# Work of the second batch ordered behind the first batch's last fold in an attention, DFT and feed-forward kernel

## The chip, the cores and the metric

The kernel runs as one program on one core of one Trainium2 chip. The metric is the device time of one execution in microseconds (us); lower is better. The core has a matrix engine (TensorE, PE in the views), a vector engine (VectorE, DVE), a scalar engine (ScalarE, ACT), a general engine (GpSimd, POOL) and an engine that here only issues transfers (SyncE, SP). Each engine carries out its own instructions in order, and engines wait for one another at semaphores.

## The reference

What is computed, for 8 batches, 12 heads, 448 tokens and 64 values per head (768 values per token):

```
q_n, k_n = rmsnorm(q, g_q), rmsnorm(k, g_k)
scores = (q_n @ k_n^T) / sqrt(64);  attn = softmax(scores);  x = attn @ v    # 12 heads side by side: 448 x 768
mixed = real(fft(fft(x, axis=tokens), axis=values))
u = x + mixed;  un = (u - mean(u)) / sqrt(var(u) + 1e-6)
out = u + relu(un @ w_ch1) @ w_ch2                                           # 768 -> 3072 -> 768
```

The two weight matrices reach the kernel as 64-bit floats and are turned into 32-bit pieces on the chip.

## The kernel before, in words

Heads are worked on two at a time: six pairs per batch. For a batch, `aux(b)` does everything ahead of the feed-forward product, as a Python generator that yields after each small step:

- `transpose_pair(b, p)` loads a pair (tile `raw`), scales it by its norm in `norm_pair` (sums of squares `ss`, a power, and two multiplies into `qkn`) and turns it by matrix transposes (`qk` in PSUM) into the tiles `QT` and `KD`. In names of tiles the pair and the part follow: `qk_1_0` is part 0 of pair 1.
- Scores `S_p_c_h`, their row extremes `mn` on DVE, exponentials `P` on ACT with row sums `sums`, transposes `pt` and `rem`, the copies `T`, the product `av` with the values, and the division (`rs`, `rt`), which ends in the transposed result `xT`.
- `fold(b, p, ...)` takes the sums and differences of pairs `p` and `p + 3` that the three-point stage of the Fourier transform needs: `eo`, `sd`, `eo` again, and, for the last fold of batch 0, six operations (two halves e = 0, 1, three each) that update the three tiles `eo_0`, `eo_1` and `tot`.
- `spectral(b, ...)`: four products `y_r_s` of 6 matmuls each from `eo_0`, `eo_1`, `tot` and a constant table; each is split into a rounded part by ACT and a rest by DVE (`Y`); then products `ab`, their sums and differences `smdf`, the residual sum `u` with statistics `st`, and the normed, transposed input `un` of the feed-forward product. `y_0_*` needs only half e = 0 for the first three of its 6 matmuls and half e = 1 for the other three; so do `y_1_*`.

`ffn(b)` then multiplies: 24 blocks `h` of 18 matmuls (L1039), each ending in `hs`, and after every four of them six blocks `o` of 12 matmuls (L1060), added into `acc`. In the first pass the weights are converted as they come in: a transfer `dbl`, two ACT operations, three DVE operations (L785, L789, L793, tile `mag`, or `mage` in the start-up), an addition on POOL (L797), a rounding copy on ACT (L802) and a DVE subtraction (L803, tiles `w`, `w2e`).

The order of work is set in three layers. While batch 0 is prepared no feed-forward work exists yet; the last lines of `spectral_block` walk through `aux(0)` and, once its list `mixing` is filled, take one step of `second = aux(1)` behind each step of it, at most `AHEAD = 14`. Afterwards `merge` mixes the rest of `aux(1)` into the first feed-forward pass in proportion to declared costs (`RATIO_FIRST`), and so on for each later batch. Last, a scheduler of the compiler, which simulates a timeline, takes this program and decides the final order on each engine and which PSUM bank a tile gets (tiles are not tied to fixed buffers here). An order can be forced on it by `order(...)`, which adds a dependency without a semaphore between two instructions of one engine. All V, A and G operations go through the recorder at L115, so they all have that line in the profile; operations of the weight conversion on DVE do not.

Of the kernel before, what the change touches and what calls it, by code (L numbers as in the profile page):

```python
# [16 lines left out]
ALU = mybir.AluOpType  # L17
# [7 lines left out]
NPAIR = H // 2  # L25
# [22 lines left out]
HALF_SCORES = range(NPAIR + 1)  # L48
PACE = 3
LAG = 3  # L50
LAST_JOINT = 2

MIN_HIGH = float(np.uint32(0x38000000).view(np.float32))
# [38 lines left out]
def spectral_block(ctx, tc, q, k, v, g_q, g_k, w1, w2, d1, d2, out, nb=B):  # L92
# [8 lines left out]
    )  # L101

    given = {}

    class Recorded:

# [4 lines left out]
        def __getattr__(self, name):  # L111
            emit = getattr(self.engine, name)

            def call(*args, **kwargs):
                ins = emit(*args, **kwargs)  # L115
                given.setdefault(ins.ins.engine, []).append(ins)
                return ins

            return call

    V, A, G = Recorded(nc.vector), Recorded(nc.scalar), Recorded(nc.gpsimd)
# [45 lines left out]
        V.tensor_tensor(out=o, in0=a, in1=b_, op=ALU.subtract)  # L167

    def add(o, a, b_):
        V.tensor_tensor(out=o, in0=a, in1=b_, op=ALU.add)  # L170

    def rows_of(n):

# [84 lines left out]
    def norm_pair(b, p):  # L258
        raw, vt = loaded.pop((b, p))
        qk = sb.tile([C, 2, NC, 2, D], F32, tag="qk", name=f"qkn{b}_{p}", bufs=1)  # L260
        sq = qk.rearrange("t i c h d -> t (i c h) d")
        flat = raw.rearrange("t i h c d -> t (i h c) d")
        nth = b * NPAIR + p
        if b < EARLY:
            A.activation(sq, flat, AF.Square)
        else:
            G.tensor_tensor(out=sq, in0=flat, in1=flat, op=ALU.mult)
        ss = sb.tile([C, 16], F32, tag="ss", name=f"ss{b}_{p}")
        V.tensor_reduce(ss, sq, axis=AX.X, op=ALU.add)
        V.tensor_scalar(  # L270
            out=ss, in0=ss, scalar1=1.0 / D, scalar2=EPS, op0=ALU.mult, op1=ALU.add
        )
        G.tensor_tensor(out=ss, in0=ss, in1=nhalf[:C], op=ALU.pow)
        for i in range(2):
            V.tensor_tensor(
                out=qk[:, i].rearrange("t c h d -> t h c d"),
                in0=raw[:, i],
                in1=ss[:, 8 * i : 8 * i + 8]
                .rearrange("t (h c) -> t h c", h=2)[:, :, :, None]
                .broadcast_to([C, 2, NC, D]),  # L280
                op=ALU.mult,
            )
        if plain(b, p):
            return qk, vt
        vhl = sb.tile([128, 4, 4, D], F32R, tag="vhl", name=f"vhl{b}_{p}", bufs=1)
        A.copy(vhl[:, :, ::3], vt)
        V.tensor_tensor(
            out=vhl[:, :, 1:3], in0=vt, in1=vhl[:, :, ::3], op=ALU.subtract
        )
        return qk, vhl  # L290
# [16 lines left out]
    def transpose_pair(b, p):  # L307

        if b >= nb or (b, p) in ready:
            return  # L310
        load_pair(b, p)
        qk, vhl = norm_pair(b, p)
        load_pair(*next_pair(b, p))
        yield 0

        if plain_s(b, p):
            T = []
            for i, tag in enumerate(("QT", "KD")):
                pt = bank(QK_BANKS[b > 0][i], f"qk{b}_{p}_{i}")
                for c in range(NC):  # L320
                    nc.tensor.transpose(
                        pt[:, c * C : (c + 1) * C],
                        qk[:, i, c].rearrange("t h d -> t (h d)"),
                        ident[:C, :C],
                    )
                t = sb.tile([128, S], F32, tag=tag, name=f"{tag}{b}_{p}")
                if i == 0:
                    A.copy(t, pt[:, :S])
                else:
                    A.activation(t, pt[:, :S], AF.Copy, scale=gneg)  # L330
                T.append(t)
                yield 420
            ready[b, p] = T[0], T[1], vhl
            return

        QT = sb.tile([128, 900], F32R, tag="QT", name=f"QT{b}_{p}")[:, : 2 * S].rearrange(
            "r (h t) -> r h t", h=2
        )
        KD = sb.tile([128, 900], F32R, tag="KD", name=f"KD{b}_{p}")[:, : 2 * S].rearrange(
            "r (h t) -> r h t", h=2  # L340
        )
        for i in range(2):
            pt = bank(QK_BANKS[b > 0][i], f"qk{b}_{p}_{i}")
            for c in range(NC):
                nc.tensor.transpose(  # L345
                    pt[:, c * C : (c + 1) * C], qk[:, i, c].rearrange("t h d -> t (h d)"),
                    ident[:C, :C],
                )
            src = pt[:, :S]
            if half_s(b, p):  # L350
                if i == 0:
                    A.copy(QT[:, 0], src)
                    sub(QT[:, 1], src, QT[:, 0])
                else:
                    A.activation(KD[:, 0], src, AF.Copy, scale=gneg)
                    V.scalar_tensor_tensor(
                        out=KD[:, 1], in0=src, scalar=gneg, in1=KD[:, 0],
                        op0=ALU.mult, op1=ALU.subtract,
                    )
            elif i == 0:  # L360
                A.copy(QT[lo, 0], src[lo])
                A.copy(QT[hi, 1], src[hi])
                sub(QT[hi, 0], src[lo], QT[lo, 0])
                sub(QT[lo, 1], src[hi], QT[hi, 1])
            else:
                for h, sl in enumerate((lo, hi)):
                    A.activation(KD[sl, h], src[sl], AF.Copy, scale=gneg[sl])
                    V.scalar_tensor_tensor(
                        out=KL[sl, h], in0=src[sl], scalar=gneg[sl], in1=KD[sl, h],
                        op0=ALU.mult, op1=ALU.subtract,  # L370
                    )
                A.copy(KD[hi, 0], KD[lo, 0].bitcast(F32))
                A.copy(KD[lo, 1], KD[hi, 1].bitcast(F32))
            yield 420

        ready[b, p] = QT, KD, vhl
# [156 lines left out]

    xTs = {}
    mixing = []

    def attention(b, EO):

# [28 lines left out]
        for n, x in enumerate(values):  # L567
            yield x
            if b == 1 and n == 4:
                fold(b, 1, xTs[b], EO)  # L570
                yield 2000
        fold(b, 2, xTs[b], EO)
        yield 3000 if b == 1 else 0


# [4 lines left out]
    def fold(b, p, xT, EO):  # L580
# [18 lines left out]
        if b == 0 and p == 2:  # L599
            for e in range(2):  # L600
# [5 lines left out]
                    out=a_, in0=two, scalar=-0.5, in1=a_, op0=ALU.mult, op1=ALU.add  # L606
                )
                sub(b_, b_, two)
                add(c_, c_, two)
            return  # L610
        twice = eo.rearrange("r i (e t) -> r (i e) t", e=2)
        add(twice[:, :, :N1], once[:, :, :N1], once[:, :, NT - 1 : N1 - 2 : -1])
        sub(twice[:, :, N1:], once[:, :, :N2], once[:, :, NT - 1 : N1 - 1 : -1])
# [142 lines left out]
    def aux(b):  # L756

        EO, uns[b] = [], {}
        yield from attention(b, EO)
        yield from spectral(b, xTs[b], EO, uns[b])  # L760
# [352 lines left out]
    load_pair(0, 0)  # L1113
    warm()
    second = aux(1)
    ahead = iter(range(AHEAD if nb > 1 else 0))
    for n, _ in enumerate(aux(0)):
        if n == DFT_STEP:
            load_dft()
        if mixing:  # L1120
            for _ in range(1):
                if next(ahead, None) is not None:
                    next(second)
        if n:
            convert_some(CONVERT_EARLY)
    starting[0] = False
# [32 lines left out]
```

## Time and profile before

| what | value |
|---|---|
| time, median of 3 runs | 2143.0 us (2142.21 to 2144.28) |
| the profiled execution: time, span of its trace | 2144.78 us, 2143.0 us |
| mean granted TensorE clock (share of full) | 0.984 |
| PE busy | 2074.9 us, 97% of the span |
| DVE busy | 1548.4 us, 72% |
| ACT busy | 1023.3 us, 48% |
| POOL busy | 342.1 us, 16% |

The span is what the trace of one execution covers; what lies around it, 1.78 us here, belongs to the time too. The busy shares are means over the whole span: in the slices of the page PE is at 7 or 8 tenths in the first four fortieths (about 214 us) and at 9 or more nearly everywhere behind them.

### The profile page before, as it was taken

Reading aid. Unit: us, or ns where it says so; the run is one execution under the profiler, and the core shown is the slowest. Engines: PE = TensorE matmul, PEld = TensorE weight load, DVE = VectorE, ACT = ScalarE, POOL = GpSimd, SP = SyncE. Lnnn points to the kernel's source line nnn. Section 1 sums busy time; section 2 is a strip of 40 time slices with the busy share of each in tenths; the row PEclk is TensorE's granted clock in tenths of the full one; section 3 lists DMA queues with packets and bytes.
Section 4 is the critical chain, followed back from the end, with each engine's and each line's share of the span. In section 5 each row is a group of like instructions: output and inputs, shape, how many; then the busy total and the mean of one; then the engine's idle time right before and its main releaser. Section 6 shows DMA issues by size and latency. Waiting matters only on the chain.

```text
span 2143.0 us, 31181 instructions
## 1 busy us (share of the span) xinstructions
PE 2074.9 (97%) x11256; PEld 1846.7 (86%) x11256; DVE 1548.4 (72%) x2948; ACT 1023.3 (48%) x2182; POOL 342.1 (16%) x182
## 2 busy tenths in 40 slices
PE   7877999999999999999999999999999999999998
PEld 4546888889999999999999999999999989999998
DVE  6788888977885878757886778858787578764122
ACT  6857876446542555335542455425553455422100
POOL 3324433311110101001110111101010011000000
PEclk9987999999999999999999999999999999999999
DMA  6538876776566855658555765667556674458874
GB/s 185 184 97 297 275 263 220 269 237 189 174 180 189 235 165 174 187 183 231 156 175 176 240 181 169 179 194 229 166 177 189 190 206 138 152 174 253 233 251 150
DMA packets 283550, 423.86 MB, mean 198 GB/s; under 512 B 181075, under 2 KB 200516, under 8 KB 283396
## 3 DMA queue, kind: packets, MB, share of 16 engines
q1 hardware_dynamic: 278962, 419.75, 63.8%
q10 hardware_dynamic: 4434, 2.11, 0.4%
q8 instruction: 90, 1.47, 0.3%
q14 instruction: 64, 0.52, 0.1%
HBM read 362.01 MB, written 65.31 MB: 199 GB/s over the span
## 4 chain that ended last, share of the span: by engine, by line
PE 81%; DVE 6%; DMA 5%; ACT 3%; issue 2%; POOL 1%; SPq 1%; DVEq 0%; POOLq 0%; ACTq 0%
PE h L1039 29%; PE o L1060 29%; PE S L409 5%; PE av L521 4%; PE pt L509 4%; DMA dbl<-w 2%; PE y L646 2%; PE qk L345 1%; DMA w<-w 1%; PE av L483 1%; DMA ur<-u_dram 1%; ACT P L115 1%; PE oT L996 1%; PE x L677 1%; PE un L908 1%
## 5 line engine op out<-in xcount | busy, mean ns | idle before, releaser
L1039 PE MATMUL h<-unT,w 128*128 128x448 f32 x3456 | 792.0, 372 | 3.4 <-DVE unT L115 1.4
L1060 PE MATMUL o<-hs,w 128*128 128x448 f32 x3456 | 786.4, 371 | 3.1 <-DVE acc L115 1.5
L1039 PEld LDWEIGHTS h<-unT,w 128*128 128x128 f32 x3456 | 638.9, 189 | 57.8 <-DVE unT L115 1.7
L1060 PEld LDWEIGHTS o<-hs,w 128*128 128x128 f32 x3456 | 635.9, 188 | 58.6 <-issue 3.4
L115 ACT ACTIVATE P<-S,mn 112x448 f32<-112x448 f32 x384 | 244.1, 638 | 232.6 <-DVE mn L115 226.7
L115 DVE TENSOR_REDUCE mn<-S 112x1 f32<-112x448 f32 x384 | 232.8, 616 | 47.9 <-PE S L409 38.3
L115 ACT ACTIVATE hs<-h 128x448 fp32r<-128x448 f32 x192 | 104.2, 543 | 299.0 <-PE h L1039 298.2
L115 DVE TENSOR_TENSOR acc<-o,acc 128x448 f32<-128x448 f32 (+1 forms) x240 | 146.9, 614 | 126.6 <-PE o L1060 125.0
L115 DVE SCALAR_TENSOR_TENSOR hs<-h,hs 128x448 fp32r<-128x448 f32 x192 | 119.0, 620 | 139.7 <-ACT hs L115 138.6
L115 POOL TENSOR_TENSOR qkn<-raw 112x1024 f32<-112x1024 f32 x36 | 68.6, 1904 | 679.3 <-PE qk L345 606.1
L115 POOL TENSOR_TENSOR ss<-ss,nhalf 112x16 f32<-112x16 f32 x48 | 142.6, 2972 | 190.2 <-DVE ss L115 167.2
L115 ACT CAST T<-pt 128x448 fp32r<-128x448 f32 x216 | 113.2, 532 | 107.3 <-PE pt L509 105.0
L521 PE MATMUL av<-T,vhl 128*128 128x448 f32 x432 | 151.0, 382 | 0.0
L115 DVE TENSOR_TENSOR T<-pt,T 128x448 fp32r<-128x448 f32 x216 | 131.4, 616 | 25.8 <-ACT T L115 24.7
L115 DVE TENSOR_SCALAR P<-P,sm 112x448 f32<-112x448 f32 x288 | 126.6, 479 | 3.8
L409 PE MATMUL S<-KD,QT 128*112 128x448 f32 x328 | 126.5, 386 | 0.6 <-ACT P L115 0.5
L509 PE MATMUL pt<-ident,P 112*128 112x112 f32 x864 | 124.8, 259 | 0.0
L409 PE MATMUL S<-rounded,QT 128*112 128x448 f32 x328 | 119.9, 366 | 0.0
L509 PEld LDWEIGHTS pt<-ident,P 112*128 112x128 f32 x864 | 103.5, 140 | 16.3 <-DVE R L115 0.3
L115 POOL TENSOR_TENSOR rstd<-st,nhalf 112x1 f32<-112x1 f32 (+2 forms) x32 | 20.2, 632 | 507.7 <-DVE st L115 507.7
L797 POOL TENSOR_TENSOR mag<-mag,dbl 128x768 uint32<-128x768 uint32 (+1 forms) x33 | 75.9, 2301 | 140.6 <-DVE mag L793 93.5
L521 PEld LDWEIGHTS av<-T,vhl 128*128 128x128 f32 x432 | 80.9, 188 | 8.3
(120 smaller groups left out, 2501.4 us busy)
## 6 DMA issues: line engine op xcount, KB each, us to landing
w<-w SPq DMA_DIRECT2D x192, 768.0 KB, 4.9
w<-w SPq DMA_DIRECT2D x288, 512.0 KB, 4.4
dbl<-w SPq DMA_DIRECT2D x20, 768.0 KB, 4.7
dbl<-w SPq DMA_DIRECT2D x13, 1024.0 KB
raw<-q SPq DMA_DIRECT2D x96, 112.0 KB, 3.8
raw<-k SPq DMA_DIRECT2D x96, 112.0 KB, 4.6
values<-v SPq DMA_DIRECT2D x96, 96.0 KB, 4.2
u_dram<-u SPq DMA_DIRECT2D x24, 336.0 KB, 3.8
```

What stands on the lines that cost most here:

```text
L115: ins = emit(*args, **kwargs)
L345: nc.tensor.transpose(pt[:, c * C : (c + 1) * C], qk[:, i, c].rearrange("t h d -> t (h d)"), ident[:C, :C],)
L409: ins = nc.tensor.matmul(s_, QT[:, h, cs], K[:, h], start=step == 0, stop=step == 1)
L483: nc.tensor.matmul(av[:, :S], vhl[:, 3 * h + j].rearrange("s h d -> s (h d)"), T, start=h + j == 0, stop=False,)
L509: nc.tensor.transpose(pt[:, c * C : (c + 1) * C], Pc[c][:, 512 * h + j * 128 : 512 * h + (j + 1) * 128], ident[:C, :C],)
L521: nc.tensor.matmul(av[:, :S], lv, T[:, i], start=(j == 0 and i == 0), stop=False)
L646: nc.tensor.matmul(o, src[:, par, t0 : t0 + n], D1[:, ri, par, cols], start=i != 1, stop=i != 0,)
L677: nc.tensor.transpose(xp[:n, i * 128 : (i + 1) * 128], src[:, 3 * half + i], ident)
L797: behind(nc.gpsimd.tensor_tensor(out=bits, in0=bits, in1=low, op=ALU.add))
L908: nc.tensor.transpose(pt[:, OFFS[i] : OFFS[i] + LENS[i]], uns[i][:, p * 128 : (p + 1) * 128], ident[: LENS[i], : LENS[i]],)
L1039: pace(nc.tensor.matmul(o, w[:, a, c], unT[c][:, z], start=n == 0, stop=n == 17))
L1060: pace(nc.tensor.matmul(o, w[:, a, f], hs[4 * g + f][:, z], start=n == 0, stop=n == 11))
```

## The change

Four things are edited.

- A dictionary `fences` holds, per engine, an instruction behind which every recorded instruction of that engine is ordered while it is set. Since `fold` now returns its last addition, which is on DVE, only DVE instructions are held.
- The loop over `aux(0)` counts the steps of `second` that it has taken. Up to `BEFORE_FOLD = 7` are taken ahead of batch 0's last fold, and the others behind it, under the fence.
- `norm_pair` becomes a generator; for the pair number `SPLIT_NORM = 7` (batch 1, pair 1, its second) it yields between the power and the two multiplies into `qkn`, so that these fall into a step of their own.
- The four tiles for converted values (slot "M") of the title are the same number in both kernels.

```diff
+SPLIT_NORM = NPAIR + 1
+BEFORE_FOLD = 7
...
             def call(*args, **kwargs):
                 ins = emit(*args, **kwargs)
+                if ins.ins.engine in fences:
+                    order(
+                        ins, fences[ins.ins.engine],
+                        mybir.DependencyClass.NoSync, mybir.DependencyReason.DATA,
+                    )
...
         G.tensor_tensor(out=ss, in0=ss, in1=nhalf[:C], op=ALU.pow)
+        if nth == SPLIT_NORM:
+            yield 0
...
-        qk, vhl = norm_pair(b, p)
+        qk, vhl = yield from norm_pair(b, p)
...
-        fold(b, 2, xTs[b], EO)
+        last = fold(b, 2, xTs[b], EO)
+        if b == 0:
+            folded.append(last)
...
+    stepped = [0]
     ahead = iter(range(AHEAD if nb > 1 else 0))
...
         if mixing:
-            for _ in range(1):
+            if folded:
+                fences[folded[0].ins.engine] = folded[0]
+            if folded or stepped[0] < BEFORE_FOLD:
                 if next(ahead, None) is not None:
+                    stepped[0] += 1
                     next(second)
+            fences.clear()
```

What the scheduler makes of it: the order of the two kernels is the same up to about the end of batch 0's attention and again from the first feed-forward pass's last `o` blocks to the end. It differs between. Three places follow. In names the prefixes are those explained above; the numbers at the end of a name only keep tiles apart.

**DVE at the fold.** First the kernel before, from the extremes of `S_0_2_0` (batch 1, pair 0) to the start of the fold's six last operations.

```order
L115 TENSOR_REDUCE mn_0_2_1310<-S_0_2_0_1311 112x1
L789 TENSOR_SCALAR mage_1270<-mage_1270 128x768
L115 TENSOR_TENSOR qkn_1_1290<-raw_1_1091,ss_1_1292 112x2x4x64 x2
L115 TENSOR_TENSOR xT_281<-rt_5_1327,xT_281 128x448
L793 SCALAR_TENSOR_TENSOR mage_1270<-dble_1271,mage_1270 128x768
L115 TENSOR_REDUCE mn_0_2_1310<-S_0_2_1_1312 112x1
L115 TENSOR_TENSOR QT_1_1370<-qk_1_0_1372,QT_1_1370 64x448 x2
...
L803 TENSOR_TENSOR w2e_1269<-mage_1270,w2e_1269 128x768
...
L115 SCALAR_TENSOR_TENSOR eo_0_998<-eo_2_1335,eo_0_998 128x2x225
L115 TENSOR_TENSOR eo_1_1182<-eo_1_1182,eo_2_1335 128x2x225
L115 TENSOR_TENSOR tot_1189<-tot_1189,eo_2_1335 128x2x225
```

Then the changed kernel: from the same place to the first `Y`.

```order
L802 TENSOR_SCALAR mage_1270<-mage_1270 128x768
L118 TENSOR_TENSOR xT_281<-rt_5_1302,xT_281 128x448
L806 SCALAR_TENSOR_TENSOR mage_1270<-dble_1271,mage_1270 128x768
L118 TENSOR_TENSOR eo_2_1310<-xT_281 128x449 x2
L118 TENSOR_TENSOR sd_2_1309<-eo_2_1310 128x2x225 x2
...
L816 TENSOR_TENSOR w2e_1269<-mage_1270,w2e_1269 128x768
L118 SCALAR_TENSOR_TENSOR eo_0_998<-eo_2_1310,eo_0_998 128x2x225
...
L118 TENSOR_TENSOR tot_1189<-tot_1189,eo_2_1310 128x2x225
L118 TENSOR_REDUCE mn_0_2_1326<-S_0_2_0_1327 112x1
L118 TENSOR_REDUCE mn_0_2_1326<-S_0_2_1_1328 112x1
L118 TENSOR_TENSOR qkn_1_1290<-raw_1_1091,ss_1_1292 112x2x4x64 x2
L118 TENSOR_TENSOR Y_0_0_1346<-y_0_0_1339,Y_0_0_1346 113x390
```

The extremes `mn_0_2` and the two multiplies `qkn_1` have moved from ahead of the fold to right behind its last addition (`tot`), and the two `QT_1` operations have left this place altogether: they stand behind batch 0's spectral part, ahead of the first feed-forward weights' subtractions.

**PE at the fold.** Before, the transposes `qk_1_0` stand ahead of `x` and `y`; the products `y_0_0` and `y_0_1` go in turns, half e = 0 first.

```order
L404 MATMUL S_0_2_1_1312<-KD_0_1131,QT_0_1130 112x448 x3
L345 MATMUL qk_1_0_1372<-ident,qkn_1_1290 128x112 x4
L677 MATMUL x_001_1438<-ident,xr_0_1430 113x128 x3
L677 MATMUL x_000_1433<-ident,xr_0_1430 113x128 x3
L646 MATMUL y_0_0_1350<-D_76,eo_0_998 113x2x65
L646 MATMUL y_0_1_1360<-D_76,eo_0_998 112x2x65
L646 MATMUL y_0_0_1350<-D_76,eo_1_1182 113x2x65
L646 MATMUL y_0_1_1360<-D_76,eo_1_1182 112x2x65
L646 MATMUL y_0_0_1350<-D_76,tot_1189 113x65
L646 MATMUL y_0_0_1350<-D_76,eo_0_998 113x2x65
```

In the changed kernel the four products come one after the other.

```order
L414 MATMUL S_0_2_1_1328<-KD_0_1131,QT_0_1130 112x448 x3
L690 MATMUL x_000_1422<-ident,xr_0_1419 113x128 x3
L690 MATMUL x_001_1427<-ident,xr_0_1419 113x128 x3
L659 MATMUL y_0_1_1349<-D_76,eo_0_998 112x2x65
L659 MATMUL y_0_1_1349<-D_76,eo_1_1182 112x2x65
L659 MATMUL y_0_1_1349<-D_76,tot_1189 112x65
L659 MATMUL y_0_1_1349<-D_76,eo_0_998 112x2x65
L659 MATMUL y_0_1_1349<-D_76,eo_1_1182 112x2x65
L659 MATMUL y_0_1_1349<-D_76,tot_1189 112x65
L659 MATMUL y_1_1_1380<-D_76,eo_0_998 112x2x65
```

`qk_1_0` is gone from here (it stands in the first `h` block now), and `y_0_1`'s second half, which needs half e = 1 of the fold, is the fourth matmul where it was the tenth.

**PE late in the first pass.** Before, the scores `S_5_3` of batch 1 stand right behind block `h_16`:

```order
L1039 MATMUL h_16_3272<-unT_5_1657,w_0_16_3000 128x448 x3
L409 MATMUL S_5_3_0_3311<-KD_5_2940,QT_5_2939 112x448
L409 MATMUL S_5_3_0_3311<-rounded,QT_5_2939 112x448
L409 MATMUL S_5_3_1_3312<-KD_5_2940,QT_5_2939 112x448
L409 MATMUL S_5_3_1_3312<-rounded,QT_5_2939 112x448
L483 MATMUL av_4_3102<-T_4_1_1_3269,values_80 128x448
L476 MATMUL pt_4_1_2_3321<-ident,P_4_0_2697 128x112
L476 MATMUL pt_4_1_2_3321<-ident,P_4_1_2784 128x112
L476 MATMUL pt_4_1_2_3321<-ident,P_4_2_2857 128x112
L476 MATMUL pt_4_1_2_3321<-ident,P_4_3_2966 128x112
L1060 MATMUL o_3_0_3329<-hs_12_2823,w_0_3_0_3040 128x448 x3
```

In the changed kernel they stand further back, the second one behind the block `o_3_0`:

```order
L355 MATMUL qk_0_0_3300<-ident,qkn_0_3187 128x112 x4
L493 MATMUL av_4_3102<-T_4_1_0_3261,values_80 128x448
L493 MATMUL av_4_3102<-T_4_1_1_3269,values_80 128x448
L486 MATMUL pt_4_1_2_3321<-ident,P_4_0_2721 128x112
L419 MATMUL S_5_3_0_3311<-KD_5_2956,QT_5_2955 112x448
...
L486 MATMUL pt_4_1_2_3321<-ident,P_4_3_2966 128x112
L1073 MATMUL o_3_0_3329<-hs_12_2823,w_0_3_0_3029 128x448 x3
L1073 MATMUL o_3_0_3329<-hs_13_3130,w_0_3_0_3029 128x448 x3
L1073 MATMUL o_3_0_3329<-hs_14_3174,w_0_3_0_3029 128x448 x3
L1073 MATMUL o_3_0_3329<-hs_15_3240,w_0_3_0_3029 128x448 x3
L419 MATMUL S_5_3_1_3312<-KD_5_2956,QT_5_2955 112x448
L419 MATMUL S_5_3_1_3312<-rounded,QT_5_2955 112x448
```

Four transposes `qk_0_0`, a product `av`, the four of `pt_4_1_2` and the 12 matmuls of `o_3_0` have passed ahead of `S_5_3_1`. On DVE the last extreme `mn_5_3` has moved likewise. Before:

```order
L115 TENSOR_REDUCE mn_5_3_3310<-S_5_3_0_3311 112x1
L115 SCALAR_TENSOR_TENSOR hs_16_3291<-h_16_3272,hs_16_3291 128x448
L115 TENSOR_REDUCE mn_5_3_3310<-S_5_3_1_3312 112x1
L803 TENSOR_TENSOR w_0_3_5_3294<-mag_3_4_3252,w_0_3_5_3294 128x512
L115 TENSOR_TENSOR eo_0_3408<-xT_1698 128x449 x2
L115 TENSOR_SCALAR sums_5_3064<-sums_5_3064 112x8
L115 TENSOR_TENSOR sd_0_3407<-eo_0_3408 128x2x225 x2
L785 TENSOR_SCALAR mag_20_3473<-mag_20_3473 128x768
L115 RECIPROCAL sums_5_3064<-sums_5_3064 112x8
L115 TENSOR_TENSOR acc_1660<-o_3_0_3329,acc_1660 128x448
```

In the changed kernel:

```order
L118 SCALAR_TENSOR_TENSOR hs_16_3291<-h_16_3272,hs_16_3291 128x448
L816 TENSOR_TENSOR w_0_3_5_3294<-mag_3_4_3244,w_0_3_5_3294 128x512
L118 TENSOR_REDUCE mn_5_3_3310<-S_5_3_0_3311 112x1
L118 TENSOR_TENSOR QT_0_3298<-qk_0_0_3300,QT_0_3298 64x448 x2
L118 TENSOR_TENSOR eo_0_3408<-xT_1687 128x449 x2
L798 TENSOR_SCALAR mag_20_3464<-mag_20_3464 128x768
L118 TENSOR_TENSOR acc_1649<-o_3_0_3329,acc_1649 128x448
L118 TENSOR_TENSOR sd_0_3407<-eo_0_3408 128x2x225 x2
L118 TENSOR_REDUCE mn_5_3_3310<-S_5_3_1_3312 112x1
```

Ahead of the last `mn_5_3` there stand now `w_0_3_5`, the two `eo_0`, one L785-type operation, `acc` and the two `sd_0` that stood behind it.

## Rows read from the trace of the kernel before

**Rows 1.** Windows: stretch, length, engines' busy us (instructions), TensorE clock, DMA share, GB/s.

```profile
130.00:144.00 14.00, 6.02 (x28) 4.96 (x29) 13.62 (x26) 6.56 (x15) 2.40 (x2) 0.58 0.46 147
144.00:152.60 8.60, 7.83 (x49) 6.62 (x48) 3.77 (x9) 3.71 (x10) 0.00 (x0) 0.90 0.00 0
152.60:177.00 24.40, 8.38 (x41) 6.91 (x41) 22.59 (x45) 17.37 (x27) 10.14 (x7) 0.64 0.58 200
185.00:355.00 170.00, 167.51 (x858) 140.58 (x857) 143.36 (x213) 132.12 (x250) 67.15 (x32) 1.00 0.82 273
355.00:440.00 85.00, 78.80 (x410) 68.73 (x409) 82.35 (x114) 43.89 (x70) 31.80 (x14) 0.98 0.66 231
```

**Rows 2.** Timeline of DVE: start, length in us, line, operation, tiles, count [idle before].

```profile
130.75 0.62 DVE L115 TENSOR_REDUCE mn<-S 112x1 f32<-112x448 f32 x1 [0.24 <-PE S L404]
131.30 0.55 DVE L789 TENSOR_SCALAR mage<-mage 128x768 uint32<-128x768 uint32 x1
131.76 1.28 DVE L115 TENSOR_TENSOR qkn<-raw,ss 112x512 f32<-112x512 f32 x2
132.97 0.62 DVE L115 TENSOR_TENSOR xT<-rt,xT 128x448 f32<-128x448 f32 x1
133.50 0.95 DVE L793 SCALAR_TENSOR_TENSOR mage<-dble,mage 128x768 uint32<-128x768 uint32 x1
134.37 0.61 DVE L115 TENSOR_REDUCE mn<-S 112x1 f32<-112x448 f32 x1
135.01 1.26 DVE L115 TENSOR_TENSOR QT<-qk,QT 64x448 fp32r<-64x448 f32 x2
136.28 1.16 DVE L115 TENSOR_TENSOR eo<-xT 128x449 f32<-128x449 f32 x2
137.48 1.17 DVE L115 TENSOR_TENSOR sd<-eo 128x450 f32<-128x450 f32 x2
...
139.43 1.29 DVE L115 TENSOR_TENSOR eo<-sd 128x226 f32<-128x226 f32 x4
...
143.33 0.62 DVE L115 TENSOR_TENSOR tot<-tot,eo 128x450 f32<-128x450 f32 x1
```

**Rows 3.** Timeline of POOL, two conversions of the start-up.

```profile
108.03 3.17 POOL L797 TENSOR_TENSOR mage<-mage,dble 128x1024 uint32<-128x1024 uint32 x1 [6.75 <-DVE sums L115]
...
134.58 1.83 POOL L797 TENSOR_TENSOR mage<-mage,dble 128x768 uint32<-128x768 uint32 x1 [4.02 <-issue]
```

**Rows 4.** Timeline of DVE beside the first of them.

```profile
108.98 3.24 DVE L115 TENSOR_TENSOR sd<-eo 128x450 f32<-128x450 f32 x2
```

**Rows 5.** Timeline of PE, first `y` and first `ab` of batch 0.

```profile
141.32 2.08 PE L646 MATMUL y<-D,eo 128*113 128x130 f32 x8 [3.20 <-DVE eo L115]
...
150.50 0.79 PE L725 MATMUL ab<-Y,rounded 113*113 113x390 f32 x3
```

**Rows 6.** Timeline of DVE, first `Y` and first `smdf`.

```profile
145.50 0.56 DVE L115 TENSOR_TENSOR Y<-y,Y 113x390 fp32r<-113x390 f32 x1 [1.55 <-ACT Y L115]
...
152.59 1.66 DVE L115 TENSOR_TENSOR smdf<-ab,bs 113x390 f32<-113x390 f32 x2
```

**Rows 7.** Timeline of PE in the first block `h`.

```profile
191.83 1.02 PE L483 MATMUL av<-T,values 128*128 128x448 f32 x2 [1.01 <-ACT T L115]
192.68 0.55 PE L476 MATMUL pt<-ident,P 112*128 112x112 f32 x4
```

**Rows 8.** Timeline of PE at the end of the first feed-forward pass.

```profile
422.94 3.84 PE L1039 MATMUL h<-unT,w 128*128 128x448 f32 x18
...
430.11 0.41 PE L908 MATMUL un<-ident,un 113*128 113x113 f32 x2 [2.26 <-ACT un L115]
431.22 5.49 PE L1039 MATMUL h<-unT,w 128*128 128x448 f32 x18 [0.70 <-DVE hs L115]
```

**Rows 9.** Window: granted clock in the last block `h` of that pass.

```profile
433.00:434.00 1.00, 1.00 (x4) 0.91 (x3) 1.00 (x2) 0.62 (x1) 0.29 (x1) 0.50 0.00 0
```

**Rows 10.** Timeline of DVE, a subtraction of the weight conversion there.

```profile
438.97 0.68 DVE L803 TENSOR_TENSOR w<-mag,w 128x512 fp32r<-128x512 f32 x1
```

More of the change, by code (lines that the diff above doesn't have):

```diff
@@ L103, in spectral_block @@
     given = {}
+    fences = {}
     class Recorded:
@@ L169, in add @@
     def add(o, a, b_):
-        V.tensor_tensor(out=o, in0=a, in1=b_, op=ALU.add)
+        return V.tensor_tensor(out=o, in0=a, in1=b_, op=ALU.add)
     def rows_of(n):
@@ L535, in spectral_block @@
     mixing = []
+    folded = []
     def attention(b, EO):
@@ L608, in fold @@
                 sub(b_, b_, two)
-                add(c_, c_, two)
-            return
+                last = add(c_, c_, two)
+            return last
         twice = eo.rearrange("r i (e t) -> r (i e) t", e=2)
```

## Prediction

> **What bounds the kernel now.** I read the page's busy shares first, then busy time by stage, then the timelines of DVE, POOL and PE where the order changes. Over the whole span PE is the bound (97% busy, the table above), but not in the stages that the change touches. In the windows [rows 1] the reader is to see who fills each stretch. From 130 to 144 us, where the last fold of batch 0 lies, DVE is busy for 13.62 of 14.00 us and PE for 6.02: DVE is the bound, instruction behind instruction. From 144 to 152.6 it is PE (7.83 of 8.60, DVE 3.77). From 152.6 to 177, the rest of the spectral part and the norm, DVE again (22.59 of 24.40). Then comes the first feed-forward pass: from 185 to 355 PE (167.51 of 170), from 355 to 440 DVE (82.35 of 85), while PE is idle for 85 − 78.80 = 6.2 us. Behind that PE is dense and the orders are the same, so what is won or lost up to some 440 us reaches the end in full.
>
> **What leaves the path ahead of the fold.** Four pieces of batch 1's work stand on DVE ahead of the fold's end [rows 2], each costed by the start of what follows it: the first `mn` 131.30 − 130.75 = 0.55 and the 0.24 us of waiting for its scores in front of it, 0.79; the two `qkn` 132.97 − 131.76 = 1.21; the second `mn` 135.01 − 134.37 = 0.64; the two `QT` 136.28 − 135.01 = 1.27. Together 3.91 us. The fold's own chain has nothing else to wait for: its operations follow one another, and its last input, `xT`, stands among them without a wait.
>
> **What comes back at once: POOL's addition.** In the kernel before, the conversion's addition on POOL starts at 134.58, right behind the third conversion step on DVE (133.50 + 0.95), and takes 1.83 us [rows 2, 3]. Beside it ran the second `mn` and the two `QT`, which read PSUM; that `mn` took 0.61 us where the first, with no addition beside it, took 0.62. Now the operations right behind the third step are `eo` and `sd` of the fold, which read two operands in SBUF. The nearest row for that is an earlier fold: its two `sd` took 3.24 us where the same pair takes 1.17 at 137.48, while POOL's 3.17 us addition began at 108.03 [rows 2 to 4]. That is 2.07 us lost. So the price here lies between 0 (the two just miss each other) and 2.07. Scaled by the lengths of the POOL operations it would be 2.07 × 1.83 / 3.17 = 1.19; if DVE stands for as long as POOL works it is 1.83. I take 1.83, since the trace's case is a stand still of most of what was left of POOL's operation (108.98 to 108.03 + 3.17 = 111.20 is 2.22 us): the fold ends 3.91 − 1.83 = 2.08 us earlier, with ends at 1.84 and 3.91.
>
> [...]
>
> **The y products.** From 141.32 to 150.50 PE runs `y`, `S_0_3` and the start of `ab` without a wait [rows 5]; this run moves with the fold. In the new order `y_0_1` needs half e = 1 as its fourth matmul. At 2.08 / 4 = 0.52 us for one `y` matmul (the row's 8 entries are 4 matmuls of two passes) PE would reach the fourth some 1.3 us after the first, at 142.6; the three operations of half e = 1 end one after another up to 143.33 + 0.62 = 143.95. The sixth matmul then starts at 143.95 and not at some 143.6. I put the cost at 0.35 us, between 0 and 0.5. The two `mn` and the two `qkn`, 0.55 + 0.64 + 1.21 = 2.4 us, lie behind the fold now, in a stretch where DVE has 8.60 − 3.77 = 4.83 us to spare and its first `Y` starts only at 145.50, 1.55 us after the fold, having waited for PE and ACT [rows 1, 6]: I cost them at nothing. Without that cover they would cost up to 2.4 − 1.55 = 0.85. The first `smdf`, at 152.59, so comes at −2.08 + 0.35 = −1.73. From there to 177 us the rows on all engines stand in the same order, and the stage moves as a whole.
>
> **Work that lands in the first pass.** The four transposes `qk_1_0` now lie in the first `h` block: at the price of four `pt`, 0.55 us, against a wait of 1.01 us for `T` in that block which shrinks by as much [rows 7]; I take nothing. The two `QT`, 1.27 us, go to a stretch where DVE has 170 − 143.36 = 26.6 us free [rows 1]. SP issues the first weight load ahead of pair 3's loads, which nothing needs before the pass; nothing.
>
> **The late scores.** On PE four `qk_0_0`, one `av`, four `pt` and 12 `o` pass ahead of `S_5_3_1`. At 0.55, 1.02 / 2 = 0.51, 0.55 and 12 × 3.84 / 18 = 2.56 us [rows 7, 8] that is 4.17 us, so the scores come at −1.73 + 4.17 = +2.4. What hangs on them is DVE, the bound of that stretch. Ahead of the last `mn_5_3` it now does five things that it did behind it: a weight subtraction 0.68 [rows 10], two `eo` 1.16, a first conversion step 0.55 (the price of the second, 131.30), `acc` 0.62 (as `xT`) and two `sd` 1.17 [rows 2]: 4.18 us. It arrives late by 2.4 with 4.2 less to do: −1.7 again. Here too I cost nothing, and the gain is handed on.
>
> **Sum.** −3.91 + 1.83 + 0.35 = −1.73 us. The sum is made against the profiled execution: its span 2143.0 becomes 2141.3, its time 2144.78 becomes 2143.05. That execution was 1.8 us above the median of the runs; the same 1.73 us taken from the median of 2143.0 gives **2141.3 us**. The case's own range is 2139.0 to 2143.0. A measurement of this kernel can tell about 0.2%, 4.3 us, from no change, so I forecast no change that can be told.
>
> **Rivals.**
>
> *DVE gives it back (12%).* The `QT` pair does not find room, because DVE's instructions go in order and wait at weights and blocks, and the DVE-bound stretch after 355 us takes it on: −1.73 + 1.27 = −0.46, 2142.5 us. For it: DVE is 97% busy there. Against it: the free 26.6 us in between.
>
> *No collision (8%).* POOL's addition falls beside the operations that read PSUM or starts late: −3.91 + 0.35 = −3.56, 2139.4 us. Against it: no operation that reads PSUM stands in the new order between the third conversion step and the fold's end.
>
> *The end of the pass closes up (22%).* At the end of the first pass PE waits 2.26 us for `un`, the normed input of batch 1, and 0.70 us for `hs`, and the last `h` block, 18 matmuls, takes 5.49 us where the block at 422.94 takes 3.84, with the granted clock at 0.50, the 1.2 GHz level, in it [rows 8, 9]. The changed kernel has `un` behind the last `h` block. If the 2.26 and 0.70 us go and with them the clock's fall, 2.26 + 0.70 + 1.65 = 4.61 us are won on top: −6.34, 2136.7 us, faster. For it: the order itself. Against it: 6.2 us of idle PE are given by DVE's work in 355 to 440 us, which stays; a wait that is taken from one place there comes up at the next one.
>
> *The last scores are late (10%, the other side).* The 4.2 us that DVE has done in advance wait in their turn (`acc` needs the `o` block, which PE reaches only now), so that nothing is made up. The end of the attention is then 2.4 us late, PE's waits there grow by that, and one more block falls to the 1.2 GHz level at the price seen, 1.65: 2143.0 + 2.4 + 1.65 = 2147.1 us, slower. It decides as soon as less than 2.4 of the 4.18 us can be done before the scores arrive. For it: `acc`, and all that stands behind it in the new order, two `sd` with 1.17 us, need PE to have done `o_3_0`.
>
> The Trainium skill, page "TensorE: Matmul & The Clock Gate", section "HAM oscillation — how this bites in real kernels", describes this: an idle gap of PE lets its clock fall, and the next burst starts at the low one. The last `h` block above, slow behind its two waits, agrees with it.
>
> **Chances and range.** The forecast has 48%. Faster by over 0.2% is the closing of the pass, 22%, with a little of the case without collision: 24%. Slower is the late scores, 10%. The rest, 66%, is within 0.2%. The range holds the forecast, the two small rivals and most of the closing: 2136.2 (half a us below its 2136.7) to 2145.5 (the forecast with half of the late scores' 1.73 + 2.4 + 1.65 = 5.8 us, rounded up); about 15% stays outside, most of it above.
>
> **What would show it.** In the changed trace the last `tot` addition should end near 141.9 and not 143.95, with one of the `eo` or `sd` pairs behind the third conversion step stretched to 2.5 to 3 us beside a POOL addition of 1.8 us. The first `smdf` should start near 150.9, the first `h` block 1.7 us earlier than now. From 185 to 355 PE should be as dense as before; at 440 us the same work should be done 1.7 us sooner. If the fold ends at 140, there was no collision; if the first pass ends more than 4 us early, the end closed up. The prediction is wrong if the fold's gain is there and does not reach the end, if the `mn` and `qkn` push `Y_0_0` back, or if the attention's end and the clock behind it move by more than the fold does.

## The result: 2157.5 us, slower by 0.64%

The changed kernel takes 2157.51 us (median of 5 runs, 2156.56 to 2158.71); the kernel before took 2144.03 in the 5 runs compared with them. The ratio is 1.0064 with a 95% interval of 1.0051 to 1.0078: slower by 13.5 us where 1.7 us less were forecast, and outside the range. The profiled execution took 2156.7 us, its span is 2154.8.

The busy times come first (page of the changed kernel). Each engine carries out as many instructions as before; beside the table of before, DVE's 1548.4 us have become 1558.7, 10.3 us more for the same 2948 instructions.

```profile
PE 2079.8 (97%) x11256; PEld 1849.9 (86%) x11256; DVE 1558.7 (72%) x2948; ACT 1023.1 (47%) x2182; POOL 345.2 (16%) x182
```

The windows of [rows 1] in the changed kernel, with the one behind them (columns as there):

```profile
130.00:144.00 14.00, 7.14 (x33) 5.45 (x33) 12.71 (x21) 5.92 (x12) 4.41 (x2) 0.63 0.35 122
144.00:152.60 8.60, 7.84 (x50) 7.12 (x50) 5.01 (x10) 4.19 (x11) 0.00 (x0) 0.80 0.24 53
...
185.00:355.00 170.00, 160.36 (x799) 132.59 (x798) 145.25 (x200) 122.53 (x229) 70.05 (x31) 0.98 0.78 257
355.00:440.00 85.00, 78.50 (x400) 67.14 (x399) 74.30 (x100) 44.01 (x77) 25.71 (x11) 0.97 0.66 216
440.00:460.00 20.00, 18.52 (x95) 16.29 (x95) 17.15 (x32) 10.14 (x17) 6.39 (x4) 0.98 0.63 236
```

Up to 177 us little has changed. In the first feed-forward pass, from 185 to 355, PE is busy for 160.36 us and not 167.51, and its granted clock is 0.98; from 440 to 460 it is busy for 18.52 us, where before it was busy for all 20.00:

```profile
440.00:460.00 20.00, 20.00 (x120) 18.30 (x120) 12.72 (x34) 9.41 (x22) 1.08 (x2) 1.00 0.89 291
```

At the fold the forecast holds. DVE's timeline (third conversion step, the pairs `eo` and `sd`, the last `tot`, the first `smdf`) and POOL's:

```profile
133.32 0.95 DVE L806 SCALAR_TENSOR_TENSOR mage<-dble,mage 128x768 uint32<-128x768 uint32 x1
134.18 2.79 DVE L118 TENSOR_TENSOR eo<-xT 128x449 f32<-128x449 f32 x2
...
137.01 1.17 DVE L118 TENSOR_TENSOR sd<-eo 128x450 f32<-128x450 f32 x2
...
142.99 0.62 DVE L118 TENSOR_TENSOR tot<-tot,eo 128x450 f32<-128x450 f32 x1
...
153.34 1.59 DVE L118 TENSOR_TENSOR smdf<-ab,bs 113x390 f32<-113x390 f32 x2
```

```profile
134.40 2.09 POOL L810 TENSOR_TENSOR mage<-mage,dble 128x768 uint32<-128x768 uint32 x1 [2.08 <-ACT xr L118]
...
373.72 3.39 POOL L118 TENSOR_TENSOR qkn<-raw 112x1024 f32<-112x1024 f32 x1 [7.71 <-PE qk L355]
377.07 1.86 POOL L810 TENSOR_TENSOR mag<-mag,dbl 128x768 uint32<-128x768 uint32 x1
```

This execution is already 1.76 us behind that of before at 131.7 us, where the orders have not yet parted (the first `mage` step starts at 131.72, before at 129.96). The last `tot` ends at 143.61 and not 143.95, so the fold has gained 2.10 us on what precedes it; 2.08 was forecast. POOL's addition collides with DVE as expected: the two `eo` take 2.79 us, 1.63 more than in [rows 2]. The first `smdf` has 1.01 us of the gain left (153.34 − 152.59 = +0.75, less 1.76).

Then the loss. PE's waits in the pass, four of the larger ones (timeline of PE):

```profile
226.17 0.41 PE L486 MATMUL pt<-ident,P 112*128 112x112 f32 x2 [1.25 <-DVE xT L118]
...
229.16 0.62 PE L419 MATMUL S<-KD,QT 128*112 128x448 f32 x1 [1.46 <-ACT P L118]
...
345.58 0.72 PE L419 MATMUL S<-KD,QT 128*112 128x448 f32 x1 [2.94 <-ACT KD L118]
...
384.86 1.02 PE L493 MATMUL av<-T,values 128*128 128x448 f32 x2 [2.09 <-ACT T L118]
```

and three windows around them:

```profile
225.00:235.00 10.00, 7.38 (x29) 6.30 (x30) 9.06 (x14) 8.23 (x16) 5.14 (x2) 0.83 0.94 315
340.00:350.00 10.00, 7.06 (x33) 5.85 (x32) 9.84 (x14) 6.58 (x12) 5.64 (x2) 0.83 0.86 283
380.00:390.00 10.00, 7.87 (x31) 5.83 (x31) 9.90 (x17) 5.49 (x9) 2.05 (x1) 0.83 0.80 283
```

Before, PE had no wait between 195 and 265 us, and none above 0.3 us between 270 and 365. Now it waits for `xT`, `P`, `KD` and `T` of batch 1's attention, and in each of these windows the granted clock falls (0.83 as a mean over 10 us: a stretch at the 1.2 GHz level and the rest at 2.4). Behind the wait at 345.58 it reads 0.50:

```profile
346.00:347.00 1.00, 1.00 (x4) 0.87 (x4) 0.94 (x3) 0.98 (x3) 0.89 (x2) 0.50 1.10 283
```

From the first `h` to the last `u` of batch 1's spectral part the pass took 448.82 − 176.96 = 271.9 us before and takes 466.02 − 177.80 = 288.2. Summed over windows of 4 us up to the end of that `u`, PE's idle time in it has grown from 10.0 to 18.9 us and its loss to the lower clock (busy time times one minus the granted clock) from 4.1 to 9.4 (2 of the 16.3 us are in neither).

What a wait hangs on can be followed back. First the last of the four, with DVE and ACT ahead of it (timelines):

```profile
366.23 0.62 DVE L118 TENSOR_REDUCE mn<-S 112x1 f32<-112x448 f32 x1 [0.68 <-PE S L419]
...
371.43 0.62 DVE L118 TENSOR_REDUCE mn<-S 112x1 f32<-112x448 f32 x1
...
375.24 3.72 DVE L118 TENSOR_SCALAR sums<-sums 112x8 f32<-112x8 f32 x1
```

```profile
382.18 0.63 ACT L118 ACTIVATE KD<-qk,gains 64x448 fp32r<-64x448 f32 x1 [1.50 <-DVE rounded L118]
...
384.28 0.97 ACT L118 COPY T<-pt 128x448 f32<-128x448 f32 x2
```

`sums` on DVE has 8 columns and takes 0.17 us undisturbed (at 152.97 us); here it takes 3.72. It stands (at work by the profile, without getting on) while POOL works at `qkn` (to 377.11) and at the conversion's addition right behind it (to 378.93), and goes on when that ends. The `rounded` product behind it is late, ACT waits 1.50 us for it before `KD`, its copy `T` comes behind that, and PE waits 2.09 us for `T`.

Ahead of the first two waits DVE stands as well. Two of its conversion operations, 0.55 and 0.95 us long undisturbed, lie beside POOL's additions and in front of the `xT` and of the row extreme that `P` needs:

```profile
221.10 2.24 DVE L798 TENSOR_SCALAR mag<-mag 128x768 f32<-128x768 f32 x1
...
226.03 1.78 DVE L816 TENSOR_TENSOR w<-mag,w 128x768 fp32r<-128x768 f32 x1
```

```profile
220.54 2.37 POOL L810 TENSOR_TENSOR mag<-mag,dbl 128x768 uint32<-128x768 uint32 x1 [8.57 <-DMA values<-v]
225.15 1.84 POOL L810 TENSOR_TENSOR mag<-mag,dbl 128x768 uint32<-128x768 uint32 x1 [2.24 <-DVE mag L806]
```

The third and longest wait, 2.94 us for `KD`, does not lead back to a stand at once. ACT, in front of its last step for `KD`, waits for a weight transfer to land:

```profile
344.04 0.90 ACT L797 ACTIVATE dbl<-dbl 128x768 uint32<-128x768 uint32 x1 [1.80 <-DMA dbl<-w]
```

The last two `mn_5_3`, at 366.23 and 371.43, are 14.7 and 18.9 us later than before (351.49 and 352.56), not 2.4.

### The profile page after: what moved, and what is told of

It reads as the page before. It is cut to its first block, busy times and chain, and to the rows that moved or that the text cites. A ratio compares the mean times of both kernels' runs of the same rounds, so it can differ in the third digit from the quotient of the medians.

```text
span 2154.8 us, 31172 instructions
## 1 busy us (share of the span) xinstructions
PE 2079.8 (97%) x11256; PEld 1849.9 (86%) x11256; DVE 1558.7 (72%) x2948; ACT 1023.1 (47%) x2182; POOL 345.2 (16%) x182
## 4 chain that ended last, share of the span: by engine, by line
PE 85%; DVE 6%; DMA 4%; ACT 2%; issue 1%; POOL 1%; SPq 0%; DVEq 0%; POOLq 0%; ACTq 0%
PE h L1052 30%; PE o L1073 30%; PE S L419 6%; PE av L531 4%; PE pt L519 4%; DMA dbl<-w 2%; PE y L659 2%; PE av L493 2%; PE qk L355 1%; PE oT L1009 1%; PE x L690 1%; PE un L921 1%; PE rem L474 1%; PE av L536 1%; DMA raw<-k 1%
## 5 line engine op out<-in xcount | busy, mean ns | idle before, releaser
L118 DVE TENSOR_TENSOR T<-pt,T 128x448 fp32r<-128x448 f32 x216 | 131.7, 617 | 25.8 <-ACT T L118 24.6
```

## Experiments

The theory after this: the pass has got longer by the order in which the scheduler now has batch 1's work in it, not by the work at the fold (**theory P**; in a second form, by how late the scores stand). Rivals: the work held back at the fold makes batch 1 late whatever the order behind it (**F**); any new order is slower than that of before, whatever the edit (**L**); and, for the means by which an order costs time, DVE's standing beside POOL (**C**). Intervals are of the ratio to the kernel before, run on the same chip.

**The two halves of the order apart.** Two kernels have the issue order of every engine written out up to the end of the first pass, by dependencies without a semaphore as the kernel's own `order` sets them; the table of instructions (`ISSUE`) and the imports are left out here.

```diff
+def pin(nc, tc):
...
+    at = {i.name: i for i in nc.cur_bb.bb.instructions}
+    for names in json.loads(zlib.decompress(base64.b85decode(ISSUE.replace("\n", "")))).values():
+        for first, then in zip(names, names[1:]):
+            tc.add_manual_dep(
+                at[f"I-{then}"], f"I-{first}",
+                mybir.DependencyInfo(
+                    mybir.DependencyClass.NoSync, mybir.DependencyReason.DATA
+                ),
+                reason="issue order",
+            )
```

In the first of them the kernel's own rule that puts batch 1's scores behind the latest feed-forward matmul is switched off, since the table says it all.

> The changed kernel's order on every engine up to the first feed-forward block (the fold, mn_0_2, qkn_1 as the change has them), and from there the order of the kernel before, written out instruction by instruction; qk_1_0 and QT_1 stand where the change has them, qk_1_1 half a block later. Theory P (the loss is made in the first pass, by where batch 1's work stands among the feed-forward blocks): the loss is gone, 2141 to 2144 us, with the fold's end 2 us earlier than before in the trace. Rival F (batch 1's DVE work that was held back at the fold is late from then on, whatever the order behind it): 2152 us or more. Rival L (any other order of the pass than that of before is slower, by luck of the scheduler's draw) expects the same as P here.

Measured: 2141.39 us (11 runs), ratio 0.9995 (0.9986 to 1.0004). Its fold and its pass:

```profile
132.30 2.79 DVE L118 TENSOR_TENSOR eo<-xT 128x449 f32<-128x449 f32 x2
...
141.11 0.62 DVE L118 TENSOR_TENSOR tot<-tot,eo 128x450 f32<-128x450 f32 x1
```

```profile
185.00:355.00 170.00, 165.97 (x846) 138.60 (x845) 145.35 (x213) 131.57 (x251) 65.52 (x32) 1.00 0.81 267
355.00:440.00 85.00, 78.84 (x405) 68.75 (x405) 82.01 (x114) 44.16 (x70) 31.78 (x14) 0.96 0.66 232
```

> The kernel before up to the first feed-forward block, with qk_1_0 and QT_1 done there, and from there the changed kernel's order on every engine, written out. Theory P: slow, 2153 to 2158 us, with PE waits in the first pass at the same places as in the changed kernel. Rival F: 2143 us, since nothing was held back. Rival L: slow as P.

Measured: 2160.55 us, ratio 1.0086 (1.0073 to 1.0100), above the 2153 to 2158 that P gave. PE has the four waits again, for `xT` (0.99 us), `P` (1.45), `KD` and `T`:

```profile
343.89 0.71 PE L409 MATMUL S<-KD,QT 128*112 128x448 f32 x1 [3.33 <-ACT KD L115]
...
384.61 1.02 PE L483 MATMUL av<-T,values 128*128 128x448 f32 x2 [2.07 <-ACT T L115]
```

F falls, and P (or L) stands: the changed start-up costs nothing, the changed pass costs all and more, 18 us.

With the changed start-up and the pass of before, the last `tot` ends at 141.73 and the first `h` starts at 175.01, 1.95 us earlier than before; but the pass takes 274.8 us where it took 271.9. So the fold's gain is real, and it is used up by the end of the pass: PE is busy for 1.5 us less from 185 to 355, and its granted clock from 355 to 440 is 0.96 where it was 0.98. Which work takes it up was not followed.

**The lost step, and the place of the scores.** By its extra yield the split needs one step more, and the step with `qk_1_0` falls out of the start-up. Batch 1's scores then stand later among the feed-forward matmuls: `S_1_0_0` (the first scores of pair 1) behind 72 of them, before behind 36.

```diff
-AHEAD = 14
+AHEAD = 15
```

> The changed kernel with AHEAD = 15 in place of 14: the fence and the split stay, and the step with qk_1_0, which the split had pushed out of the start-up into the first pass, is taken in the start-up again (still behind the fold). S_1_0_0 stands behind 36 feed-forward matmuls again, as before, and not behind 72; the scheduler makes its own order. Theory P in its form with the lost step: 2141 to 2146 us. Rival F: 2155 us or more. Rival L: somewhere between 2145 and 2160, with no relation to where the scores stand.

Measured: 2148.39 us, ratio 1.0027 (1.0016 to 1.0039): slower than P's range, within L's.

```diff
-                fences[folded[0].ins.engine] = folded[0]
+                pass
...
-BEFORE_FOLD = 7
+BEFORE_FOLD = 99
```

> The changed kernel without the fence and without the limit of seven steps: only the extra yield in norm_pair, which costs the start-up its step with qk_1_0. S_1_0_0 stands behind 56 feed-forward matmuls. Theory P with the lost step: slower than before, 2149 to 2158 us. Rival F: 2143 us. Rival L: 2145 to 2160.

Measured: 2150.69 us, ratio 1.0044 (1.0031 to 1.0057): F falls again, P and L both allow it.

```diff
-BEFORE_FOLD = 7
+BEFORE_FOLD = 14
```

> The changed kernel with BEFORE_FOLD = 14 in place of 7: nothing is kept from the start-up's loop ahead of the fold any more, the fence and the split stay. The scheduler's order of the start-up and of the pass differs from both kernels, but S_1_0_0 stands behind 72 feed-forward matmuls, as in the changed kernel. Theory P in its form 'the later batch 1's scores stand, the longer the pass': 2153 to 2160 us. Rival L (any new order costs, with no relation to the scores' place): anywhere from 2145 to 2160.

Measured: 2148.56 us, ratio 1.0029 (1.0018 to 1.0041): faster than P's second form allows.

```diff
-AHEAD = 14
+AHEAD = 17
```

> The changed kernel with AHEAD = 17 in place of 14: two more steps of batch 1 in the start-up than the kernel before had. The scores of pair 1's last tile stand behind 90 feed-forward matmuls (before 102, with AHEAD = 15 106, changed kernel 138). Theory P: 2138 to 2145 us, not slower than before and faster than with AHEAD = 15, unless the start-up grows. Rival L: 2145 to 2160.

Measured: 2158.24 us, ratio 1.0074 (1.0061 to 1.0086), far above the 2138 to 2145 that P gave; P's exception, a longer start-up, is what happened. PE's timeline shows where: the first `h` is late.

```profile
186.72 0.74 PE L1052 MATMUL h<-unT,w 128*128 128x448 f32 x1 [0.96 <-ACT unT L118]
```

Its pass takes 460.89 − 186.72 = 274.2 us, nearly as little as before, with two steps less to do in it; but the start-up has grown by 9.8 us.

The first pair looked like a rule (36, 56 and 72 matmuls: 2148, 2151 and 2158 us), and the second pair broke it: 72 matmuls and 2149 us in bf14. P in its second form falls. What is left is that each small edit gave another order of the pass, and that these took longer: from the first `h` to the last `u` 280.3 us in split_only, 280.8 in ahead15, 279.4 in bf14, 288.2 in the changed kernel, and 271.9 before.

**An edit that has nothing to do with the fold.** The kernel before, with

```diff
-RATIO_FIRST = 0.6
+RATIO_FIRST = 0.605
```

> The kernel before with RATIO_FIRST = 0.605 in place of 0.6: the start-up and the fold are as before, the scheduler's order of the first pass differs from some 200 feed-forward matmuls on. Theory L (each new order of the pass meets other collisions, whatever the edit was for; that of before is a good one): slower than before by 4 to 16 us, 2147 to 2159. If the loss needs the fence, the split or late scores: 2139 to 2146.

Measured: 2151.10 us, ratio 1.0036 (1.0022 to 1.0050). Neither fence nor split nor a later `S_1_0_0`, and 7.5 us are lost: L holds for this edit, the one of its kind that was tried. Its pass takes 457.70 − 178.72 = 279.0 us.

**What makes an order cost.** Both kernels' orders written out, with POOL's addition cut to 8 columns. (No run has an order written out and nothing else changed. The nearest are the two mixed ones above, whose ratios, 0.9995 and 1.0086, lie near those of the kernels whose pass they have, 1 and 1.0064.)

```diff
-        behind(nc.gpsimd.tensor_tensor(out=bits, in0=bits, in1=low, op=ALU.add))
+        few = (slice(None), slice(0, 1), slice(0, 8))
+        behind(nc.gpsimd.tensor_tensor(
+            out=bits[few], in0=bits[few], in1=low[few], op=ALU.add
+        ))
```

> The changed kernel's order on every engine, written out, with POOL's addition of the weight conversion done on 8 columns of a tile only; left out is the low part of the other weights. Beside the run b_small_add. If the collisions of DVE with POOL's additions make the waits of the first pass (theory C), most of the 18 us between the two orders goes: difference to b_small_add under 6 us. If the place of the scores makes them and collisions only ride along, the difference stays at 10 us or more.

> The kernel before's order on every engine, written out, with the same cut of POOL's addition (left out is the low part of all but 8 columns of each weight tile). By itself it shows what the additions cost this kernel: 2130 to 2143 us, since DVE is the bound of the end of the pass and stands for some 28 us beside POOL in it.

Measured: 2124.58 us with the changed order (ratio 0.9913, 0.9900 to 0.9927) and 2126.37 with that of before (0.9924, 0.9912 to 0.9937). The difference between the orders is gone (theory C), and the bound given for the kernel before was too timid. This cut also brings the converted weights sooner and leaves POOL idle, so a third pair keeps POOL busy and its result late. What it computes is no conversion (see the expectation):

```diff
-        behind(nc.gpsimd.tensor_tensor(out=bits, in0=bits, in1=low, op=ALU.add))
+        few = ident[:, : 9 if c * f == 768 else 13]
+        behind(nc.gpsimd.tensor_tensor(
+            out=value[:, 0, : few.shape[1]], in0=few, in1=few, op=ALU.pow
+        ))
```

> The changed kernel's order on every engine, written out, with each of POOL's additions of the weight conversion replaced by a power on POOL that is meant to take about as long but reads and writes 9 or 13 columns only (left out are the low parts of the weights, and those columns become 1). Beside the run b_pow. Theory C1 (DVE stands because both engines stream large tiles of SBUF at once): the collisions are gone though POOL is as busy and its result as late; a_pow and b_pow both at 2122 to 2132 us, less than 6 us apart. Theory C2 (what the small additions gave back was the waiting for POOL's result, not the standing of DVE): times stay near 2140 and 2155, 8 us or more apart.

> The kernel before's order on every engine, written out, with the same powers in place of POOL's additions. C1: 2122 to 2132 us. C2: 2138 to 2143 us.

Measured: 2127.91 us (0.9926, 0.9914 to 0.9939) and 2127.61 us (0.9929, 0.9916 to 0.9941). All powers came out with 13 columns. POOL's groups in the pass (columns: line, engine, operation, tiles, shapes, count, busy us, mean ns, idle before), first the additions of the changed kernel, then the powers in its order:

```profile
L810 POOL TENSOR_TENSOR mag<-mag,dbl 128x768 uint32<-128x768 uint32 x18 | 37.5, 2088 | 68.3 <-DVE mag L806 40.8 <-DMA values<-v 8.6 <-DMA dbl<-w 6.9
L810 POOL TENSOR_TENSOR mag<-mag,dbl 128x1024 uint32<-128x1024 uint32 x13 | 35.1, 2704 | 60.9 <-DVE mag L806 27.9 <-ACT mag L796 14.7 <-ACT w L815 7.8
```

```profile
L811 POOL TENSOR_TENSOR mag<-ident 128x13 f32<-128x13 f32 x30 | 82.7, 2759 | 101.1 <-DVE mag L806 61.9 <-ACT mag L796 13.2 <-ACT hs L118 6.7
```

POOL is busier with the powers (82.7 us against 37.5 + 35.1) and each takes as long as the longest additions. Yet the pages of a_pow and b_pow read:

```profile
PE 2067.0 (97%) x11256; PEld 1844.5 (87%) x11256; DVE 1518.3 (71%) x2948; ACT 1023.3 (48%) x2182; POOL 358.9 (17%) x182
```

```profile
PE 2065.7 (97%) x11256; PEld 1844.8 (87%) x11256; DVE 1517.9 (72%) x2948; ACT 1023.5 (48%) x2182; POOL 354.6 (17%) x182
```

DVE needs 1518.3 and 1517.9 us: 40 us less than in the changed kernel, 30 less than before, and the 10.3 us between the two orders are gone with the 13.5 us of time.

So it is DVE's standing (C1) that makes an addition costly and not the waiting for its result (C2). Two things ride along: the power is another operation than the addition, and it does not read `dbl`, whose buffer is so free one operation sooner. Neither was tried by itself. Of PE's four waits the one for `KD`, which did not lead back to a stand, is still there in a_pow, behind a `dbl` transfer again:

```profile
329.89 0.46 PE L419 MATMUL S<-KD,QT 128*112 128x448 f32 x1 [2.06 <-ACT KD L118]
```

The waits for `xT` and for `P` ahead of the scores are gone, and none for `T` is over 0.8 us; one of 1.6 us, for `P` ahead of `rem`, is new.

**A version that is faster than both.** The order of new_start_old_pass, with each addition in two halves:

```diff
-        behind(nc.gpsimd.tensor_tensor(out=bits, in0=bits, in1=low, op=ALU.add))
+        for cut in (slice(0, c // 2), slice(c // 2, c)):
+            behind(nc.gpsimd.tensor_tensor(
+                out=bits[:, cut], in0=bits[:, cut], in1=low[:, cut], op=ALU.add
+            ))
```

> The order of the run new_start_old_pass (the changed start-up, the pass of the kernel before) with each of POOL's additions made in two halves, computing everything. If DVE, once it meets an addition, stands until that instruction ends, shorter instructions cost it less: the 28 us of standing in the pass fall to some 15 to 20 and the time to 2132 to 2139 us, faster than both kernels. If POOL and DVE lose the same time piece by piece: 2139 to 2145 us.

Measured: 2138.03 us (11 runs), ratio 0.9977 (0.9968 to 0.9986), 5 us faster than before and near the upper end of the first range. Its page:

```profile
PE 2070.5 (97%) x11256; PEld 1845.1 (86%) x11256; DVE 1540.9 (72%) x2948; ACT 1023.1 (48%) x2182; POOL 354.7 (17%) x224
```

POOL works 12 us longer than in new_start_old_pass (342.6), and DVE 10 us less (1550.8 there). The halving by itself is the step from 0.9995 to 0.9977, some 4 us; the two ratios were measured on different chips.

## Why the prediction was wrong

- **The bound of each stage, and the four pieces ahead of the fold:** right. That what is lost by 440 us "reaches the end in full" is right only in the main: at the last `u` the profiled execution is 17.2 us behind that of before, at its end 11.9. The fold ends 2.10 us earlier in the changed kernel and 2.1 in new_start_old_pass (141.73 against 143.95, where the first `mage` step starts 0.12 us earlier).
- **POOL's addition beside the fold:** right in kind, mis-sized by little: 1.63 us on `eo` where 1.83 was taken. So far the trace agrees with the Trainium skill, page "SBUF — State Buffer", section "Who interferes with whom", by which a DVE instruction with two SBUF inputs contends with a GpSimd instruction that reads SBUF: `eo` has its two operands there, and the pair stands for 1.63 us beside an addition of 2.09.
- **The `y` products:** not settled. At the first `smdf` 1.01 us of the gain are left in the changed kernel's execution, 2.06 in that of new_start_old_pass (150.41 against 152.59, less the 0.12), with the same order up to there; 1.73 was forecast. So the products cost 1.09 us in the one and 0.04 in the other, where 0.35 was taken, between 0 and 0.5. What differs in the rows is the granted clock, 0.80 and 1.00 in the window from 144 to 152.6. The `mn` and `qkn` behind the fold cost nothing, as forecast: DVE waits 2.91 us for ACT ahead of its first `Y`.
- **"Work that lands in the first pass" and "The late scores":** here the prediction failed. Both were costed at nothing, from places in the order and undisturbed durations: 2.4 us late with 4.2 us less to do, hence no loss. That sum has no term for who runs beside whom, and it looks at three places of an order that differs all along the pass: of the 411 DVE instructions between the two ends that both kernels share, at least 127 stand elsewhere (from the two traces, by operation, tiles and shape). The runs show 16.3 us more for the pass instead. It is late well ahead of the scores that were priced: the 253rd `h` matmul starts at 346.10 us and not at 333.52. The orders put other DVE operations beside POOL's additions; DVE is busy for 10.3 us more in all; in three of the four waits shown such a stand lies ahead of what PE waits for, and behind the waits the clock is down. With the powers in place of the additions the loss is gone. The prediction had priced just this collision, for one addition at the fold, and not for the 31 additions of the pass among which DVE's work is reordered.
- **The rivals:** the side was named (the attention late, PE waiting, the clock falling), but with the wrong place and too small a price: one wait at the end of the pass, 2147.1 us. Whether DVE gives the fold's gain back (the rival of 2142.5 us) can't be told: new_start_old_pass, at 0.9995 (0.9986 to 1.0004), allows the forecast (0.9992) and this rival (0.9998) alike. DVE is no busier there from 355 to 440 than before (82.01 against 82.35 us), which speaks against the rival's reason.
- **The range:** its upper end is not the sum that it names. The forecast with half of 5.8 us on top is 2144.2, not 2145.5; the measured time lies far above either.

What stays open: which of the collisions cost an order its time. Their sum does not rank the orders. DVE's busy time is 1550.8 us in rf61, no more than in new_start_old_pass, and rf61 is 10 us slower. Only the orders of the changed kernel and of before were run with the powers, so whether rf61's loss would go with them is not shown. Nor was it tried whether the changed order with halved additions gains more than that of before.

## What to carry to other kernels

An edit of a kernel whose order a scheduler makes is two edits: the one that was meant, and a new draw of all that follows. Hold the order behind the edit fixed to see the first alone (here 1 us, no more than the measurement can tell from none), and compare with an edit that means nothing to see the second (here 7.5 us lost). When you cost a new order, ask of every stretch which engines now run beside one another, and not only how long each operation takes alone. Where two engines stop one another, the length of the one's instructions is a setting: two halves in place of a whole gave some 4 us.

## What the runs showed of the hardware

A DVE operation of 8 columns (`sums`, 0.17 us alone) stood for 3.55 us through the rest of one POOL instruction and the whole of the next. It has one operand, in SBUF; so has the `mag` at 221.10 us that took 2.24 us beside an addition and takes 0.55 undisturbed. Two operands in SBUF are thus not needed for a stand.

How long POOL's instruction is does not decide it alone. With powers of 2.76 us on 13 columns in place of the additions DVE was busy for 1518 us; additions of 2.09 and 2.70 us over 768 and 1024 columns cost it 30 to 40 us more, though the powers read SBUF too. The changed kernel shows the same by its own powers, 16 columns each (`ss`): beside one of them a DVE operation with two operands of 1024 columns takes 1.22 us, as it does alone (1.23 at 327.52 us).

```profile
387.95 3.47 POOL L118 TENSOR_TENSOR ss<-ss,nhalf 112x16 f32<-112x16 f32 x1 [9.02 <-DVE ss L118]
```

```profile
389.24 1.22 DVE L806 SCALAR_TENSOR_TENSOR mag<-dbl,mag 128x1024 uint32<-128x1024 uint32 x1
```

Whether the few columns or the operation itself spares DVE is not shown: the POOL instructions that were seen to spare it were powers, or the additions of 8 columns, which took under half a us.
